# A fused attention and maxout kernel: batch 0 takes its h undivided by the sums, its weights in fp16, a recut tail of the first pass, and the next batch's h one burst later

## The chip, the cores and the metric

The kernel runs on one core of one Trainium2 chip. Time is device microseconds (us) of one execution on that core; quoted are medians with the lowest and highest of the runs. The core is TensorE (matmul), VectorE (DVE), ScalarE (ACT), GpSimd (POOL), SyncE (SP) and DMA engines.

## The reference, cut to what matters

```python
# x: [4, 12544, 128], inducing: [32, 128], w1, w2: [128, 1024], w_out: [1024, 128]
def mab(q, kv):
    s = scale * (q @ kv.transpose(0, 2, 1))        # scale = 1/sqrt(128)
    a = np.exp(s - s.max(-1, keepdims=True))
    a /= a.sum(-1, keepdims=True) + 1e-09
    return a @ kv
h = mab(I, x)                 # 32 rows per batch, from all 12544 tokens
y = mab(x, h)                 # each token attends to the 32 rows
out = np.maximum(y @ w1, y @ w2) @ w_out
```

The kernel works with max(a, b) = a + relu(b - a). So y @ w1 @ w_out becomes the attention weights times `m1 = h @ (w1 @ w_out)`, and y @ (w2 - w1) the attention weights times `hwd = h @ (w2 - w1)`. Both are small and made once a batch. In the code E is exp of the scores of the first pass, and h = (sum of E x) / (sum of E).

## The kernel before

The first batch (batch 0) is read in units of up to 16 tiles of 128 tokens: transposes, scores, exp, accumulation of E sums and of h. Then comes a long stream of bursts (hidden layer) and finals (output). The next batch's first pass runs as jobs between the bursts.

```python
    units = []
    for i, (_, n) in enumerate(p1_blocks):
        step = 8 if i == NP1 - 2 else n
        units += [(i, g, min(step, n - g)) for g in range(0, n, step)]
    units = units[:-3] + units[-1:] + units[-3:-1]
    NU = len(units)
    # ... pools, loads of x, transposes of x, u_scores (scores of a unit, exp on ScalarE) ...
        def u_accum(i):
            t, g, n = units[i]
            et = pool0.pop(("et", i))
            xn = xn_of(0, t)
            if i == 0:
                for name in ("h", "sum"):
                    pool0[name] = bank([128, 512])
                    model.bank_free[pool0[name][0]] = 1e9
            for j in range(0, n, 4):
                w = min(4, n - j) * M
                nc.tensor.matmul(
                    out=pool0["sum"][1][:, 0:w],
                    lhsT=ones16,
                    rhs=et[:, j : j + w // M, :],
                    start=(i == 0 and j == 0),
                    stop=(i == NU - 1 and j + 4 >= n),
                )
                model.pe(0.056)
            for j in range(n):
                nc.tensor.matmul(
                    out=pool0["h"][1][:, 0:M],
                    lhsT=xn[:, g + j, :],
                    rhs=et[:, j, :],
                    start=(i == 0 and j == 0),
                    stop=(i == NU - 1 and j == n - 1),
                )
                model.pe(0.025)

        def u_h():
            rec = smp.tile([C, M], F32, name="hrec_0", tag="hrec")
            nc.vector.reduce_sum(
                out=rec,
                in_=pool0["sum"][1][:, 0 : 4 * M].rearrange("p (k m) -> p m k", k=4),
                axis=mybir.AxisListType.X,
            )
            nc.vector.reciprocal(out=rec, in_=rec)
            hT4 = smp.tile([C, 4, M], F16, name="hT4_0", tag="hT4")
            nc.vector.tensor_mul(
                hT4,
                pool0["h"][1][:, None, 0:M].broadcast_to((C, 4, M)),
                rec[:, None, :].broadcast_to((C, 4, M)),
            )
            end = model.ev("DVE", 256 + 128, model.t["PE"], 0.2)
            for name in ("h", "sum"):
                model.bank_free[pool0[name][0]] = end
            st[0]["hT4"] = hT4.rearrange("c q m -> c (q m)")
        # ... scores and accumulation of the later batches, E summed on GpSimd ...
        def small_fold(b):
            acc = st[b]["eacc"]
            n = P1B // 2
            while n:
                nc.gpsimd.tensor_add(out=acc[:, 0:n, :], in0=acc[:, 0:n, :], in1=acc[:, n : 2 * n, :])
                n //= 2
            st[b]["esum"] = acc[:, 0, :]

        def small_h(b):
            es = st[b]["esum"]
            bi, ps = bank([128, 512])
            nc.tensor.matmul(out=ps[:, 0:M], lhsT=ones32, rhs=es, start=True, stop=True)
            end = model.pe(0.11, model.bank_free[bi])
            rec = smp.tile([C, M], F32, name=f"hrec_{b}", tag="hrec")
            nc.vector.reciprocal(out=rec, in_=ps[:, 0:M])
            hT4 = smp.tile([C, 4, M], F16, name=f"hT4_{b}", tag="hT4")
            nc.vector.tensor_mul(
                hT4,
                st[b]["hacc"][:, None, :].broadcast_to((C, 4, M)),
                rec[:, None, :].broadcast_to((C, 4, M)),
            )
            model.bank_free[bi] = model.ev("DVE", 256 + 128, end, 0.2)
            st[b]["hT4"] = hT4.rearrange("c q m -> c (q m)")

        def small_hwd(b):
            hwd = smp.tile([128, J], F16, name=f"hwd_{b}", tag="hwd")
            w = 256 if b == 0 else 512
            for i in range(J // w):
                bi, ps = bank([128, 512])
                sl = slice(w * i, w * (i + 1))
                nc.tensor.matmul(
                    out=ps[:, 0:w], lhsT=st[b]["hT4"], rhs=w21[:, sl], start=True, stop=True
                )
                end = model.pe(w / 2400 + 0.002, model.bank_free[bi])
                if i % 2 == 0:
                    nc.vector.tensor_copy(out=hwd[:, sl], in_=ps[:, 0:w])
                    model.bank_free[bi] = model.ev("DVE", w, end)
                else:
                    nc.scalar.copy(out=hwd[:, sl], in_=ps[:, 0:w])
                    model.bank_free[bi] = model.ev("ACT", w, end)
            st[b]["hwd"] = hwd
        # ... small_m1: m1 = hT4 x w1out, copied by ScalarE, m1d on GpSimd ...
        # ... Block.stage: scores against hT4, exp by ScalarE with the constant scale;
        #     burst: 16 matmuls of e2 against hwd, relu by DVE or ScalarE;
        #     final: relu against woutp (with m1d first), multiply by 1/denominator on DVE, store ...
        def prep_w1T():
            for g in range(2):
                bi, ps = bank([128, 512])
                for j in range(4):
                    jb = 4 * g + j
                    nc.tensor.transpose(
                        ps[:, 128 * j : 128 * (j + 1)],
                        w1f[:, 128 * jb : 128 * (jb + 1)],
                        identity32,
                    )
                    end = model.pe(0.12, model.bank_free[bi])
                nc.scalar.copy(out=w1T[:, 4 * g : 4 * g + 4, :], in_=ps)
                model.bank_free[bi] = model.ev("ACT", 512, end)
        # ...
        last = NU - 3
        for i in range(last - 1):
            u_transpose(i)
            if i >= 1:
                u_accum(i - 1)
            u_scores(i)
            keep_warm(1)
        u_transpose(last - 1)
        u_accum(last - 2)
        u_transpose(last)
        u_transpose(last + 1)
        u_scores(last - 1)
        u_transpose(last + 2)
        u_accum(last - 1)
        u_scores(last)
        u_scores(last + 1)
        u_scores(last + 2)
        for i in range(last, NU):
            u_accum(i)
        for i in range(NXN - NP1):
            load_x(1, i)
        u_h()
        for i in range(4):
            eng = nc.vector if i == 3 else nc.gpsimd
            sl = slice(256 * i, 256 * (i + 1))
            eng.tensor_sub(w21[:, sl], w2f[:, sl], w1f[:, sl])
        for i in range(NXN - NP1, NP1):
            load_x(1, i)
        prep_w1T()
        # ... blocks, stages ...
        stages[-1][0].stage()
        small_hwd(0)
        for blk in stages[-1][1:]:
            blk.stage()
        prep_w1out()
        # ... jobs: at(g, f) runs f behind burst g ...
            for s, f in ((40, small_fold), (42, small_h), (43, small_hwd), (44, small_m1)):
                at(g + s, f, nb)
```

## Time and profile before

| | before |
|---|---|
| time, median of 3 runs | 340.58 us (340.24 to 341.95) |
| span of the profiled execution | 338.5 us |
| TensorE busy | 97% |
| accumulation of batch 0 ends (called t0) | 23.62 |
| first burst on TensorE | 26.19 |
| first output multiply | 29.27 |
| TensorE dense from | 36.21 |

One can read this as a TensorE stream of about 300 us with a start in front of it. Whatever comes before the stream counts in full, and inside the stream only gaps of TensorE count. The lines for both are in the prediction. Two more views matter for the argument. The first is the list of what TensorE waited for, over the whole span of the kernel before, here the longest three of its six entries (engine line, what it waited for: us in total, times, longest):

```profile
PE ps L208 <- ACT xT L200: 1.3, 4, 0.4
PE ps L173 <- DVE warm L158: 1.2, 1, 1.2
PE ps L331 <- POOL eacc L324: 1.0, 1, 1.0
```

No wait for a DMA is in the whole list: the data of x was always there before TensorE came to it. The second view is a line of the timeline of GpSimd (start us, us, engine, line, operation, count, then the idle time before it and what ended that):

```profile
22.64 2.10 POOL L660 TENSOR_TENSOR w<-wf 128x256 f16<-128x256 f32 x3 [4.14 <-DMA wf<-in_moe_w_dram]
```

This is three quarters of w2 - w1; DVE forms the fourth. The work can't start before w2 has landed (22.50). GpSimd ends at 22.64 + 2.10 = 24.74, DVE at 25.03. The four multiplies that need one quarter each (L350) start on TensorE at 24.93, 25.04, 25.15 and 25.26, so the third quarter is 0.41 us early and the fourth only 0.23 us. I did not look at how tight this is when I predicted; the experiments come back to it.

### The profile page before, as it was taken

The numbers are of one execution on the slowest core, as the hardware profiler recorded it, in microseconds if no ns is written. First come the engines' busy times: TensorE is split into PE (matmuls) and PEld (weight loads), VectorE is DVE, ScalarE is ACT, GpSimd is POOL, SyncE is SP. The second block draws the span as 40 slices with busy tenths as digits, with TensorE's granted clock in tenths as the row PEclk, the third lists the DMA queues.
The fourth block names the chain that finished last, engine by engine and source line by source line (L and its number), as shares of the span: only waits on it lengthen the run. The fifth ranks groups of instructions, "written<-read, shape, count | busy, mean of one in ns | idle before, by whom it ended". The sixth has DMA issues, their size and how long they took to land.

```text
span 338.5 us, 14493 instructions
## 1 busy us (share of the span) xinstructions
PE 329.7 (97%) x6346; PEld 263.8 (78%) x6346; DVE 295.9 (87%) x620; ACT 269.7 (80%) x521; POOL 92.9 (27%) x164
## 2 busy tenths in 40 slices
PE   8899999999999999999999999999999999999996
PEld 3787688888768878888777878887777777878875
DVE  1348999999989999999998999999998998989994
ACT  1559988777888887787899777877899989888881
POOL 7243113454532224443242141423242100000000
PEclk9999999999999999999999999999999999999999
DMA  7999799499719985994229951212221221222222
GB/s 130 211 270 214 193 244 255 131 193 232 203 64 181 275 180 129 195 244 141 88 95 205 273 174 65 95 71 90 96 95 67 100 99 72 95 96 95 97 97 108
DMA packets 53423, 50.42 MB, mean 149 GB/s; under 512 B 41456, under 2 KB 42128, under 8 KB 53360
## 3 DMA queue, kind: packets, MB, share of 16 engines
q0 software_dynamic: 11408, 33.43, 37.0%
q1 hardware_dynamic: 41952, 16.08, 21.9%
q8 instruction: 49, 0.80, 1.0%
q14 instruction: 14, 0.11, 0.1%
HBM read 27.28 MB, written 25.69 MB: 157 GB/s over the span
## 4 chain that ended last, share of the span: by engine, by line
PE 93%; ACT 3%; DVE 1%; POOL 1%; issue 1%; DVEq 0%; POOLq 0%
PE ps L544 56%; PE ps L471 19%; PE ps L486 4%; PE ps L297 2%; PE ps L275 2%; PE ps L406 2%; PE ps L173 2%; PE ps L192 2%; ACT relu L508 1%; ACT xT L200 1%; PE ps L208 1%; PE ps L427 1%; PE ps L350 1%; DVE relu L504 1%; POOL eacc L324 1%
## 5 line engine op out<-in xcount | busy, mean ns | idle before, releaser
L508 ACT ACTIVATE relu<-ps 128x512 f16<-128x512 f32 x444 | 235.5, 601 | 43.0 <-PE ps L471 29.7
L504 DVE TENSOR_SCALAR relu<-ps 128x512 f16<-128x512 f32 x340 | 218.7, 679 | 5.3 <-PE ps L471 4.5
L544 PE MATMUL ps<-woutp,relu 128*128 128x128 f16 x3136 | 209.1, 220 | 0.0
L544 PEld LDWEIGHTS <-relu 128*128 128x128 f16 x3136 | 176.4, 98 | 29.8 <-issue 20.2
L560 DVE TENSOR_TENSOR o<-ps,rp 128x256 f32<-128x256 f32 x196 | 81.9, 418 | 16.0 <-PE ps L544 14.2
L570 POOL DMA_DIRECT2D out_dram<-o x75 | 41.1, 547 | 156.4 <-DVE o L560 108.1
L471 PE MATMUL ps<-e,hwd 32*128 32x256 f16 (+1 forms) x1632 | 82.8, 268 | 0.4
L471 PEld LDWEIGHTS <-hwd 32*128 32x128 f16 x1632 | 27.0, 92 | 19.0 <-issue 3.2
L486 PE MATMUL ps<-m,e 32*128 32x128 f16 x372 | 29.7, 214 | 0.7
L486 PEld LDWEIGHTS <-e 32*128 32x128 f16 x372 | 18.2, 92 | 7.0 <-issue 3.9
L317 POOL TENSOR_TENSOR eacc<-eacc,et 128x512 f32<-128x512 f32 (+1 forms) x18 | 18.5, 1028 | 0.3
L284 ACT ACTIVATE et<-ps 128x512 f16<-128x512 f32 (+1 forms) x21 | 11.4, 544 | 4.8 <-PE ps L275 4.8
L416 ACT ACTIVATE e<-ps 128x512 f16<-128x512 f32 (+2 forms) x30 | 14.9, 553 | 0.0
L114 POOL DMA_DIRECT2D xn<-in_x_dram x21 | 11.5, 550 | 4.7 <-DMA xn<-in_x_dram 4.1
L197 DVE COPY xT<-ps 128x1024 f16<-128x1024 f16 (+1 forms) x8 | 5.1, 642 | 8.4 <-PE ps L192 8.4
L200 ACT COPY xT<-ps 128x1024 f16<-128x1024 f16 x5 | 5.1, 1012 | 9.0 <-PE ps L192 9.0
L275 PE MATMUL ps<-inducingT,xT 128*128 128x32 f16 x294 | 10.6, 176 | 0.0
L297 PE MATMUL ps<-et,xn 128*128 128x32 f16 x294 | 10.6, 176 | 0.0
L275 PEld LDWEIGHTS <-xT 128*128 128x128 f16 x294 | 9.6, 96 | 0.0
L297 PEld LDWEIGHTS <-xn 128*128 128x128 f16 x294 | 9.5, 96 | 0.0
L173 PE MATMUL ps<-warm 128*128 128x512 f16 x22 | 7.7, 495 | 1.2 <-DVE warm L158 1.2
L406 PE MATMUL ps<-xT,hT 128*32 128x512 f16 (+2 forms) x120 | 8.7, 350 | 0.1
(65 smaller groups left out, 115.4 us busy)
## 6 DMA issues: line engine op xcount, KB each, us to landing
out_dram<-o POOLq DMA_DIRECT2D x72, 256.0 KB, 3.2
xn<-in_x_dram POOLq DMA_DIRECT2D x23, 512.0 KB, 8.9
out_dram<-o SPq DMA_DIRECT2D x24, 256.0 KB, 2.0
wf<-in_moe_w_dram POOLq DMA_DIRECT2D x2, 512.0 KB, 13.7
xn<-in_x_dram POOLq DMA_DIRECT2D x2, 256.0 KB, 13.5
out_dram<-o POOLq DMA_DIRECT2D x3, 128.0 KB, 4.7
xT<-xn SPq DMA_TRANSPOSE x21, 6.2
xn<-in_x_dram POOLq DMA_DIRECT2D x4, 64.0 KB, 9.3
```

The source lines that it names most:

```text
L275: nc.tensor.matmul(out=ps[:, j * M : (j + 1) * M], lhsT=xT_tiles[b % 2][:, k0 + j, :], rhs=inducingT, start=True, stop=True,)
L297: nc.tensor.matmul(out=ps[:, 0:M], lhsT=xn[:, j, :], rhs=et[:, j, :], start=(j == 0), stop=(j == n - 1),)
L317: nc.gpsimd.tensor_add(out=acc, in0=acc, in1=et[:, 0:n, :])
L406: nc.tensor.matmul(out=ps[32 * q : 32 * (q + 1), 0 : self.width], lhsT=st[self.b]["hT4"][:, 32 * q : 32 * (q + 1)], rhs=xT[:, q % self.g], ...
L416: nc.scalar.activation(out=self.e2[:, 0 : self.width], in_=ps[:, 0 : self.width], func=AF.Exp, scale=scale,)
L471: nc.tensor.matmul(out=ps[:, jj * w : (jj + 1) * w], lhsT=st[blk.b]["hwd"][r, 128 * jb : 128 * (jb + 1)], rhs=blk.e2[r, 128 * self.t0 : 12 ...
L486: nc.tensor.matmul(out=part.fin[q][1][:, 128 * s : 128 * (s + 1)], lhsT=part.blk.e2[r, 128 * tt : 128 * (tt + 1)], rhs=st[part.blk.b]["m1" ...
L504: nc.vector.tensor_scalar(out=dst, in0=src, scalar1=0.0, scalar2=None, op0=ALU.max)
L508: nc.scalar.activation(out=dst, in_=src, func=AF.Relu)
L544: nc.tensor.matmul(out=o, lhsT=self.relu[:, jb, q, tt, :], rhs=woutp[:, jb, :], start=False, stop=(s == 1 and jb == NJB - 1),)
L560: nc.vector.tensor_mul(self.osb[:, h : h + 2, :], ps[:, 0:256].rearrange("p (s c) -> p s c", s=2), rp.broadcast_to((128, 2, 128)),)
L570: eng.dma_start(out=outr[blk.b, :, k : k + nst, :], in_=self.osb[:, 0:nst, :])
```

## The change

The intent is a shorter path from the last data of x to the first burst, and no stall at batch 1's fold.

- **h undivided.** Batch 0's h is only multiplied by a constant 2**-14. The division by the E sums moves to where results leave PSUM: as a [128,1] scale of the exponentials and of the evictions of hwd and m1. E sums come as a column (weights E, moving operand one column of ones) in place of 128 columns.
- **fp16 weights.** w1 and w2 are loaded into fp16 tiles. The eight transposes of w1 are fp16, run while DVE scales and copies h, and leave by one DVE copy. w2 - w1 isn't formed: each hwd bank takes h x w2 and then -h x w1. The fp32 copies that later batches need are loaded and subtracted on GpSimd inside the stream.
- **Recut tail.** The last full block of batch 0 comes as 8, 4 and 4 tiles instead of 8 and 8, and the order on TensorE changes.
- **Fold later.** Batch 1's h, hwd and m1 come one burst later.
- In a final, the m1d matmuls come last.

The diff, cut to its core (some statements are put in words):

```diff
@@ units
-        step = 8 if i == NP1 - 2 else n
-        units += [(i, g, min(step, n - g)) for g in range(0, n, step)]
-    units = units[:-3] + units[-1:] + units[-3:-1]
+        if i == NP1 - 2:
+            units += [(i, 0, n // 2), (i, n // 2, n // 4), (i, n // 2 + n // 4, n // 4)]
+        else:
+            units.append((i, 0, n))
+    units = units[:-4] + units[-1:] + units[-4:-1]
+    last = NU - 4
@@ constants and loads
-    ones16 = consts.tile([128, 128], F16, name="ones16")
+    ones16 = consts.tile([128, 1], F16, name="ones16")
+    same_m = consts.tile([128, 4, M], F32, name="same_m")   # filled from identity32 by 4 DVE copies
+    sum_scale = consts.tile([128, 2], F32, name="sum_scale")  # HS and HS / scale, HS = 2**-14
-        nc.gpsimd.dma_start(out=w1f, in_=moe_w1)
-        nc.gpsimd.dma_start(out=w2f, in_=moe_w2)
+        nc.gpsimd.dma_start(out=w1h, in_=moe_w1)              # fp16 tiles of their own
+        nc.gpsimd.dma_start(out=w2h, in_=moe_w2)
@@ u_accum: E sums come out as a column
-                    out=pool0["sum"][1][:, 0:w],
-                    lhsT=ones16,
-                    rhs=et[:, j : j + w // M, :],
+                    out=pool0["sum"][1][0:w, 0:1],
+                    lhsT=et[:, j : j + w // M, :],
+                    rhs=ones16,
@@ u_h: h is only scaled by HS; the sums become two [128,1] scales
+            nc.vector.tensor_mul(
+                part, pool0["sum"][1][:, 0:1].broadcast_to((128, 2)), sum_scale
+            )
+            w1T_bank = w1T_transpose()            # 8 fp16 transposes into one bank
+            nc.tensor.matmul(out=ps[:, 0:2], lhsT=same_m..., rhs=part, start=True, stop=True)
+            nc.vector.tensor_scalar(out=hT4, in0=h broadcast to 4, scalar1=HS, ..., op0=ALU.mult)
+            nc.vector.reciprocal(out=rs, in_=ps[:, 0:2])
+            nc.scalar.mul(neg, hT4, -1.0)
+            w1T_evict(*w1T_bank)                  # one DVE copy
+            st[0]["rs"], st[0]["scale"] = rs[:, 0:1], rs[:, 1:2]
-            (reduce_sum, reciprocal, tensor_mul on DVE)
@@ u_hwd: two matmuls a bank in place of w21 = w2 - w1
+                for lhsT, rhs, first_mm in (
+                    (st[0]["hT4"], w2h, True),
+                    (st[0]["neg"], w1h, False),
+                ): ...
+            # evictions: hwd = ps * rs, banks 0 and 1 on ScalarE, 2 and 3 on DVE
@@ small_m1, stage
-            nc.scalar.copy(out=m1, in_=ps[:, 0:128])
+            if b == 0:
+                nc.scalar.mul(m1, ps[:, 0:128], st[0]["rs"])
-                    scale=scale,
+                    scale=st[self.b]["scale"],
@@ final: the two m1d matmuls of a group come behind its 16 relu matmuls
@@ order of the start
-        (8 fp32 transposes of w1 behind u_h, 2 ScalarE copies of them)
-        for i in range(4):
-            eng = nc.vector if i == 3 else nc.gpsimd
-            sl = slice(256 * i, 256 * (i + 1))
-            eng.tensor_sub(w21[:, sl], w2f[:, sl], w1f[:, sl])
+        for i in range(last - 2):
+            u_transpose(i); (u_accum(i - 1) if i >= 1); u_scores(i); keep_warm(1)
+        u_transpose(last - 2)
+        u_accum(last - 3)
+        u_transpose(last - 1)
+        u_scores(last - 2)
+        u_transpose(last)
+        u_transpose(last + 1)
+        u_scores(last - 1)
+        u_transpose(last + 2)
+        u_scores(last)
+        u_transpose(last + 3)
+        u_scores(last + 1)
+        u_accum(last - 2)
+        u_scores(last + 2)
+        u_scores(last + 3)
+        for i in range(last - 1, NU):
+            u_accum(i)
@@ jobs
+            d = 1 if b == 0 else 0
             for s, f in ((40, small_fold), (42, small_h), (43, small_hwd), (44, small_m1)):
-                at(g + s, f, nb)
+                at(g + s + (0 if f is small_fold else d), f, nb)
+        at(24, load_wf)            # w1, w2 once more, fp32, for w21 of the later batches
+        for i in range(4):
+            at(33 + 2 * i, sub_w, i)   # w21 quarter by quarter on GpSimd
```

> **What bounds the kernel now.** I read the page first, then the timeline of all engines from 0 to 40 us, then the waits of TensorE after 26 us, then the landing time of each early DMA, issue by issue. The page says that the whole is a TensorE stream with a start in front of it:
>
> ```profile
> PE 329.7 (97%) x6346; PEld 263.8 (78%) x6346; DVE 295.9 (87%) x620; ACT 269.7 (80%) x521; POOL 92.9 (27%) x164
> PE 93%; ACT 3%; DVE 1%; POOL 1%; issue 1%; DVEq 0%; POOLq 0%
> ```
>
> From 36 us to 90 us the table by stretches has PE busy 53.99 of 54.00 us; nothing off TensorE can shorten that, and the order of instructions shows that the change leaves the stream there as it is. So only the start (up to 36 us) and stalls of TensorE later are open. The waits of TensorE from 26 us to the end hold one entry worth anything:
>
> ```profile
> 90.67 0.54 POOL L570 DMA_DIRECT2D out_dram<-o  x1 [2.40 <-DVE hacc L310]
> 91.62 1.99 POOL L324 TENSOR_TENSOR eacc<-eacc 128x256 f32<-128x256 f32 x4
> 93.66 0.41 PE L331 MATMUL ps<-eacc,ones 128*128 128x32 f32 x2 [0.97 <-POOL eacc L324]
> ```
>
> The fold of batch 1's E sums on GpSimd ends at 93.61, and the matmul that needs it sits at the head of TensorE's queue from 92.69: 0.97 us lost, once. The later batches show no such wait.
>
> The start, on TensorE (and the ScalarE copy that paces a unit of 16 tiles):
>
> ```profile
> 16.69 1.01 ACT L200 COPY xT<-ps 128x1024 f16<-128x1024 f16 x1 [0.52 <-PE ps L192]
> 17.76 0.36 PE L208 MATMUL ps<-inducingT,xT 128*128 128x32 f16 x8 [0.29 <-ACT xT L200]
> 18.19 1.05 PE L192 MATMUL ps<-identity,xn 128*128 128x128 f16 x16
> 20.26 0.55 PE L208 MATMUL ps<-inducingT,xT 128*128 128x32 f16 x16
> 20.66 0.61 PE L192 MATMUL ps<-identity,xn 128*128 128x128 f16 x8
> 23.42 0.35 PE L242 MATMUL ps<-et,xn 128*128 128x32 f16 x8
> 23.62 1.07 PE L611 MATMUL ps<-identity,wf 128*128 128x128 f32 x8
> 26.19 0.40 PE L471 MATMUL ps<-e,hwd 32*128 32x128 f16 x16
> ```
>
> A unit recurs every 2.58 us (15.60 to 18.19), paced by transposes, then a 1.01 us copy, then scores. Accumulation ends at 23.62 (call it t0); the first burst starts at 26.19, 2.57 us later. From there to about 36 us evictions set the pace; ScalarE hardly stops:
>
> ```profile
> 27.02 1.09 ACT L508 ACTIVATE relu<-ps 128x512 f16<-128x512 f32 x2
> 27.99 0.41 ACT L416 ACTIVATE e<-ps 128x256 f16<-128x256 f32 x1
> 28.25 1.12 ACT L508 ACTIVATE relu<-ps 128x512 f16<-128x512 f32 x2
> 29.54 3.54 ACT L508 ACTIVATE relu<-ps 128x512 f16<-128x512 f32 x7 [0.16 <-PE ps L471]
> 32.94 1.11 ACT L416 ACTIVATE e<-ps 128x512 f16<-128x512 f32 x2
> 34.04 4.76 ACT L508 ACTIVATE relu<-ps 128x512 f16<-128x512 f32 x9
> ```
>
> x lands (issue time plus time to landing, each issue asked alone): fifth load 17.2, the two-tile one 17.55, the two halves of the last 18.8 and 20.1; w1 21.2, w2 22.5, w_out 23.9. A consumer starts some 0.2 us later.
>
> **What the Trainium skill says.** "TensorE: Matmul & The Clock Gate", Back-to-back issue gap: N/2.4 + 2.5 ns warm, with a floor near 25 ns for small N. The trace agrees: four sums of 128 columns take 11.32 to 11.54 (55 ns each), sixteen 32-column matmuls 11.54 to 11.95 (26 ns each). "ScalarE: Activation LUTs", What ACT_TABLE_LOAD costs: each [128,1] pointer operand adds about 93 ns to an ACTIVATE. Nothing in this trace has a scale of that kind, so it can't be checked before; it matters, since the change gives such a scale to the exponentials, the hwd evictions and m1 of batch 0. "DMA: Bandwidth & Descriptors", Where 436 GB/s comes from: a ceiling of 435 GB/s. x loads land 2.45 us apart for 1.05 MB of fp32 read, 428 GB/s, so x can't come earlier, and fp16 weights, still read as fp32, can't either: 0.52 MB in about 1.25 us both ways.
>
> **The change part by part.**
>
> Schedule of the last units. The loop now stops after three units and the last 16 tiles come as 8, 4, 4. I place its TensorE order on the trace's times with 56 ns a transpose, 25 ns a small matmul, 0.69 us a DVE copy of 8 tiles. The sum matmul falls from 55 to 25 ns (0.12 us a unit), but in the paced units that only widens the 0.29 us wait for the copy. Accumulation of unit 2 ends at 16.99, so the fifth unit's transposes wait for their data: 17.4 to 18.3, against 18.19 before. Scores of the fourth unit 18.3 to 18.7; two tiles to 18.81; eight tiles 19.0 to 19.45 (landed 18.8); scores of the fifth 19.48 to 19.88 (DVE, now copying both halves, is done at 19.42); four tiles to 20.10; two-tile scores 20.15; last four tiles 20.3 to 20.52 (landed 20.1); eight scores to 20.72; accumulation of the fourth unit (20 matmuls) to 21.22, scores to 21.42, the remaining accumulation of 34 tiles 1.08 us: t0 = 22.50. Against 23.62: **1.12 us** gained, about half from the transposes starting earlier and half from 25 cheaper sums and a gapless tail. The four new same_m copies delay the first DVE copy by an estimated 0.6 to 0.8 us (from 0.17 us of a small copy each), but its scores wait for ScalarE until 10.00 anyway, and the 0 to 0.2 us left vanish in the wait for data at 17.4.
>
> From t0 to the first burst. Removed: reduce, reciprocal, multiply on DVE (23.62 to 24.70) before anything could start; eight fp32 transposes (1.07); two ScalarE copies of w1T (1.07); the subtraction. Added on TensorE, in order: eight fp16 transposes 0.45, one fp32 matmul about 0.30 (the pair at 93.66 held TensorE 0.34), scores 0.18, eight hwd matmuls of 256 columns 0.86 (four before), second scores 0.18, eight w1out 0.45. Sum 2.42 against 2.57. The chain beside it: part 0.17, matmul result at t0+0.85, reciprocal to t0+1.05, exp to 1.5, two ScalarE hwd evictions to 2.3, DVE w1T copy 0.69 and two hwd evictions to 2.54; the third pass of the burst needs that at 2.6. So TensorE work replaces the wait: **0.15 us**, first DVE relu at t0+2.85 against t0+3.02. On ScalarE hwd, the second exp, w1out and m1, each with a pointer, put the first relu at t0+3.56 against t0+3.40. In all, 0.
>
> Start of the stream. Four scaled activations (m1, three exps before 34 us) at 0.09 us add up to 0.36 us to a ScalarE that doesn't stop; DVE is near as full. I count 0.15 us lost. m1d matmuls last in a final: its group waits for relu anyway (28.06 after 27.99), so 0.
>
> Fold one burst later. A burst and its final take 1.3 to 1.5 us; 92.69 + 1.4 = 94.1, after the fold's 93.61. The four 0.72 us subtractions move to GpSimd between bursts 33 and 39, where it idles 1.0 to 2.4 us at a time, so the fold isn't late: **0.97 us** gained whole.
>
> Sum: 1.12 + 0 - 0.15 + 0.97 = 1.95 us, so 340.58 - 1.95 = 338.6 us.
>
> **The rivals.** First, x's arrival takes the place of TensorE's order: the last four tiles land at 20.1, and if quarter loads land later by 0.5 us, t0 moves to 23.0 and the time to 339.1. Against it: they are read at the same rate. Second, ScalarE becomes the bound from t0 to 36 us, because every pointer costs its full 0.09 us and m1 comes later: 0.5 us more, 339.1. For it: the lines from 27.02 on. Third, the gain on the path is larger, with DVE setting the first evictions (0.17 us) and the pointers hidden behind overlap of back-to-back activations: 338.2. Fourth, the fold stall comes back at the new place because the subtractions or the second weight load hold GpSimd up: 339.5. The idle times before 90.67 speak against it. Fifth, the transposes of batch 1 by DMA: they wait for x that lands at 39.1 while the step now comes at 39.0, scores at 45.6 need a transpose that takes 4.6 us from 39.5: about 1.4 us of slack, no cost.
>
> **Range and chances.** Rivals one, two and four in part together leave a gain of about 0.9; the good ends together give 2.9. I take 337.7 to 339.7. Two per cent is 6.8 us, beyond anything in the start, so faster by that 0.01, within 0.985, slower 0.005.
>
> **What would show it.** Fifth unit's transposes near 17.4; first w1T transpose near 22.5; first burst at 24.9, TensorE without a gap before it; ScalarE's first relu near 26.0; no TensorE wait for the fold. A t0 above 23, a new DMA wait before the last transposes, or scaled exps holding banks so that the stream gets dense later than 35.3 would make it wrong.

## The result, and the profile after

| | before | after |
|---|---|---|
| time, median of 6 runs each of the same rounds | 340.92 us (340.24 to 341.95) | 339.04 us (338.44 to 339.95) |
| ratio | | 0.9945 (95% interval 0.9923 to 0.9966) |
| span of the profiled execution | 338.5 us | 336.9 us |
| t0 | 23.62 | 22.69 |
| first burst | 26.19 | 25.38 |
| first output multiply | 29.27 | 28.54 |
| TensorE dense from | 36.21 | 35.49 |

A ratio is the mean time of one kernel's fast runs over that of the other's fast runs of the same rounds, so not quite the ratio of the medians that I quote. All runs were in the fast state. The verdict is "same" at 2%. The medians lie 1.88 us apart, the predicted difference was 1.95 us, and 339.04 lies in the predicted range.

The chain of work that ended last, from the changed kernel's page:

```profile
PE 90%; DMA 4%; POOL 1%; ACT 1%; DVE 1%; issue 1%; POOLq 0%
```

DMA is new in that chain with 4% of 336.9 us, about 13 us: the start is now followed back to the loads of x and not to ScalarE, which had 3% before. The list of TensorE's waits in the changed kernel says the same (its entries for `warm` and `mask`, which the kernel before has too, are left out):

```profile
PE ps L218 <- DVE xT L207: 1.1, 1, 1.1
PE ps L218 <- ACT xT L210: 0.8, 2, 0.4
PE ps L202 <- DMA xn<-in_x_dram: 0.6, 1, 0.6
PE ps L555 <- ACT relu L592: 0.4, 2, 0.2
```

The wait for the fold is gone from it, a wait for x has come. The 1.1 us for a DVE copy is in the first unit and lies in front of that wait for x, so it costs nothing. It comes from the four new same_m copies, which took 0.91 us at 7.70 in front of that copy (0.6 to 0.8 were predicted).

The start of the changed kernel, from the timeline of TensorE:

```profile
17.38 1.07 PE L202 MATMUL ps<-identity,xn 128*128 128x128 f16 x16 [0.65 <-DMA xn<-in_x_dram]
...
22.69 0.61 PE L264 MATMUL ps<-identity,w1h 128*128 128x128 f16 x8
23.14 0.34 PE L283 MATMUL ps<-sum_part,same_m 128*128 128x2 f32 x2
23.51 0.24 PE L490 MATMUL ps<-xT,hT 128*32 128x128 f16 x4
23.68 0.28 PE L399 MATMUL ps<-w2h,hT 128*128 128x256 f16 x1
...
24.83 0.62 PE L699 MATMUL ps<-woutp,w1T 128*128 128x128 f16 x8
25.38 0.40 PE L555 MATMUL ps<-e,hwd 32*128 32x128 f16 x16
```

The fifth unit's transposes come as its data does, at 17.38 (17.4 was predicted). t0 is the first transpose of w1, at 22.69. From there to the first burst TensorE is hardly idle, and still takes 25.38 - 22.69 = 2.69 us, more than the 2.57 us before. In those 2.69 us the eight transposes run to 23.14, the fp32 matmul of the sums and an idle moment behind it (see e8_tuned) last to 23.51, the eight hwd matmuls run to 24.66 (0.98 us), the second scores to 24.83, w1out to 25.38 (0.55 us).

The fold of batch 1 in the changed kernel, on GpSimd and TensorE, and below it the burst that followed the fold's matmul in the kernel before:

```profile
90.97 1.99 POOL L364 TENSOR_TENSOR eacc<-eacc 128x256 f32<-128x256 f32 x4
92.38 1.07 PE L619 MATMUL ps<-woutp,relu 128*128 128x128 f16 x16
93.29 0.36 PE L371 MATMUL ps<-eacc,ones 128*128 128x32 f32 x2
93.58 0.40 PE L555 MATMUL ps<-e,hwd 32*128 32x256 f16 x8
```

```profile
94.00 0.40 PE L471 MATMUL ps<-e,hwd 32*128 32x256 f16 x8
```

The fold ends at 90.97 + 1.99 = 92.96. The matmul that needs it now stands behind one more burst and final and starts at 93.29, with no idle time before it. From the start of the final ahead of the fold's matmul to the burst behind it, the changed kernel takes 93.58 - 92.38 = 1.20 us; the kernel before took 94.00 - 91.63 = 2.37 us for the same work. That is 1.17 us, more than the 0.97 us that the profile calls idle, because an idle time is counted from a modelled end of the matmuls.

To see where the time went I compare the start of every output multiply on DVE, of which each kernel has 196, one against the other (after less before):

| output multiply (numbered from 0) | time before | difference |
|---|---|---|
| 0 | 29.27 | -0.73 |
| 34 | 87.01 | -0.72 |
| 38 | 92.96 | -0.68 |
| 44 | 104.30 | -1.86 |
| 101 | 193.99 | -1.81 |
| 195 (last) | 335.35 | -1.95 |

There are two steps and no more. 0.72 us come from the start, and 1.86 - 0.68 = 1.18 us from the place of the fold. The last -0.14 is not the change's: the profile of the kernel before hesitates once at about 196 us (multiply 102), and the traces of e1_fold to e4_schedfold below hold the same -0.15 or so against it there, whatever they change. The span shrinks by 1.6 us only, since the last store ended 3.5 us behind the last multiply after and 3.1 us before.

### The profile page after: what moved, and what is told of

Same layout as the page of the kernel before. It is cut to its first block, busy times and chain, and to the rows that moved or that the text cites. A ratio compares the mean times of both kernels' runs of the same rounds, so it can differ in the third digit from the quotient of the medians.

```text
span 336.9 us, 14513 instructions
## 1 busy us (share of the span) xinstructions
PE 327.8 (97%) x6351; PEld 262.9 (78%) x6351; DVE 296.7 (88%) x627; ACT 269.6 (80%) x521; POOL 94.4 (28%) x166
## 3 DMA queue, kind: packets, MB, share of 16 engines
q1 hardware_dynamic: 42240, 17.13, 25.7%
## 4 chain that ended last, share of the span: by engine, by line
PE 90%; DMA 4%; POOL 1%; ACT 1%; DVE 1%; issue 1%; POOLq 0%
PE ps L619 57%; PE ps L555 19%; PE ps L570 4%; DMA xn<-in_x_dram 4%; PE ps L337 2%; PE ps L315 2%; PE ps L490 2%; ACT relu L592 1%; POOL xn L123 1%; DVE o L645 1%; PE ps L511 1%; DVE relu L588 1%; PE ps L252 0%; PE ps L431 0%; PE ps L628 0%
## 5 line engine op out<-in xcount | busy, mean ns | idle before, releaser
L207 DVE COPY xT<-ps 128x1024 f16<-128x1024 f16 (+2 forms) x10 | 5.7, 596 | 6.8 <-PE ps L202 6.6
L500 ACT ACTIVATE e<-ps 128x512 f16<-128x512 f32 (+1 forms) x21 | 10.9, 581 | 0.0
L210 ACT COPY xT<-ps 128x1024 f16<-128x1024 f16 x4 | 4.0, 1012 | 7.8 <-PE ps L202 7.8
L490 PE MATMUL ps<-xT,hT 128*32 128x512 f16 (+2 forms) x120 | 8.7, 350 | 0.0
L202 PE MATMUL ps<-identity,xn 128*128 128x128 f16 x98 | 6.9, 219 | 1.0 <-DMA xn<-in_x_dram 0.6
```

Source lines behind the costliest of these rows:

```text
L490: nc.tensor.matmul(out=ps[32 * q : 32 * (q + 1), 0 : self.width], lhsT=st[self.b]["hT4"][:, 32 * q : 32 * (q + 1)], rhs=xT[:, q % self.g], ...
```

## The experiments

The theory was: (1) the fold's place alone gives about 1 us or a little more; (2) the start gives some 0.7 us, and what sets it is the arrival of x, the order on TensorE behind it, and then TensorE's own work up to the first burst. Rivals: the gain comes from the rewritten arithmetic alone or the new cut alone; the [128,1] scales cost their full length; the order in the final matters. Differences in us below are (1 - ratio) times the median of the kernel before of the same call. In the first call that median was 340.35 us (340.10 to 340.82, 11 runs), in the second 340.74 (340.22 to 342.26, 11 runs), in the fourth, on a noisier chip, 341.48 (340.30 to 343.04, 11 runs). Some runs have a mean granted clock of 0.995 or less and are 0.5 to 4 us longer than their like: two of the 11 of the kernel before in the second call (342.21 and 342.26) and in the fourth (342.72 and 343.04), two of e11_split's six, and one each of e8_tuned's and e12_tunedsplit's. They count as fast, and are in the ratios. In the second call they raise the mean of the kernel before, and with it every difference, by 0.27 us.

This table gathers what the traces show of each kernel's start. "Multiply 0" and "195" are the times of the first and last output multiply against the same trace of the kernel before.

| kernel | first transposes | t0 | first burst | t0 to burst | multiply 0 | 195 |
|---|---|---|---|---|---|---|
| before | 7.84 | 23.62 | 26.19 | 2.57 | 0 | 0 |
| after | 7.19 | 22.69 | 25.38 | 2.69 | -0.73 | -1.95 |
| e1_fold | 8.09 | 23.88 | 26.45 | 2.57 | +0.26 | -1.07 |
| e2_nofold | 7.05 | 22.70 | 25.46 | 2.76 | -0.64 | -0.76 |
| e3_sched | 8.65 | 23.09 | 25.93 | 2.84 | -0.27 | -0.39 |
| e4_schedfold | 8.27 | 22.72 | 26.00 | 3.28 | -0.20 | -1.53 |
| e5_rewrite | 7.08 | 22.80 | 25.59 | 2.79 | -0.51 | -1.80 |
| e6_nosub | 8.24 | 22.68 | 25.35 | 2.67 | -0.84 | -1.54 |
| e7_imm | 8.37 | 22.83 | 25.80 | 2.97 | -0.40 | -1.68 |
| e8_tuned | 6.70 | 22.44 | 25.39 | 2.95 | -0.72 | -1.95 |
| e9_after | 7.90 | 22.71 | 25.97 | 3.26 | -0.14 | -1.37 |
| e10_m1dfirst | 8.30 | 22.80 | 25.75 | 2.95 | -0.35 | -0.36 |
| e11_split | 8.49 | 23.76 | 27.81 | 4.05 | +1.70 | +1.27 |
| e12_tunedsplit | 6.89 | 23.19 | 25.77 | 2.58 | -0.34 | -1.57 |

The second column must be read first. The warming matmuls at the head of the kernel run at a lower rate until the clock opens, 376 to 634 ns for one and the same 512-column matmul in one trace, and when it opens differs from run to run. The traces' granted clock becomes 1.00 at 4.24 us in after, 5.55 in before and 7.19 in e3_sched, and over the 12 traces with 18 warming matmuls the first transposes follow in the same order, between 7.05 and 8.65 (7.19 and 7.90 in two traces of the same changed kernel). The 6.70 and 6.89 of e8_tuned and e12_tunedsplit have 14 warming matmuls. In the kernel before TensorE paces all that follows: t0 comes 15.78 us behind the first transposes in before (23.62 - 7.84) and 15.79 in e1_fold (23.88 - 8.09). In the changed kernel t0 stays at 22.69 to 22.83 over five traces (after, e2, e7, e9, e10) with first transposes from 7.05 to 8.37: its early units have idle time that takes up a late start, and its fifth unit waits for x when the start was early (0.65 us in the first trace, 0.27 in e9's, none in e7's and e10's). So the pair before and after is not a fair one: the clock opened 1.31 us sooner in after. The fair pair is before and e9_after, whose clock opened at 5.66.

### e1_fold: the fold's place alone

The kernel before with only this:

```diff
+            d = 1 if b == 0 else 0
             for s, f in ((40, small_fold), (42, small_h), (43, small_hwd), (44, small_m1)):
-                at(g + s, f, nb)
+                at(g + s + (0 if f is small_fold else d), f, nb)
```

> Kernel before with nothing changed but batch 1's sums used one burst later. Theory (the removed wait of 0.97 us and a second one right behind it are worth 1.1 us of the 1.9): 1.1 us faster than before, TensorE waits nowhere for the fold, the start is as before. Rival (the gain is all in the start; the wait is made up later, since TensorE runs in a regime where evictions had got ahead): 0.0 to 0.3 us faster.

Measured: 338.94 us (338.80 to 339.26, 5 runs), ratio 0.9960 (0.9948 to 0.9971), 1.36 us faster. In its trace the wait for the fold is gone: the fold ends at 91.87 + 1.99 = 93.86 and the matmul starts at 94.21. The multiplies go from +0.25 ahead of the fold to -0.94 behind it, a step of 1.19 us, the same as the changed kernel's. So the fold's step is shown to stand by itself.

### e2_nofold: the change without the fold's new place

```diff
-            d = 1 if b == 0 else 0
+            d = 0
```

> Changed kernel with the sums of batch 1 used at the old burst again. Theory: 1.0 to 1.2 us slower than the changed kernel, so 0.7 to 0.9 us faster than before; a wait of about 1 us at the fold's matmul comes back. Rival (start is everything): within 0.3 us of the changed kernel, 1.6 to 1.9 us faster than before.

Measured: 340.08 us (339.41 to 340.70, 6 runs), ratio 0.9991 (0.9978 to 1.0004), 0.3 us faster, which can't be told apart from no change and is less than both texts expected. The list of TensorE's waits has the old one back:

```profile
PE ps L371 <- POOL eacc L364: 1.0, 1, 1.0
```

In its trace the start gains 0.64 us, in the mean of its runs 0.3. The trace had its first transposes at 7.05, and a kernel before that starts as early should gain with it (no run shows one); a single pair of traces therefore says too much or too little about the start, and the mean over runs is the better judge.

### e3_sched: the new cut and order alone

The kernel before with the hunks of the units and of the order of the start, and nothing else:

```diff
-    units = units[:-3] + units[-1:] + units[-3:-1]
+    units = units[:-4] + units[-1:] + units[-4:-1]      # last block as 8, 4, 4
+    (order of transposes, scores and accumulation as in the change)
```

> Kernel before with the new cut (8, 4, 4) and order of the last units alone; h divided as before, sums of 128 columns. Theory (the start's gain of 0.7 us is the schedule): fifth unit's transposes near 17.4 us, accumulation ends near 23.0 to 23.1, first burst near 25.6 to 25.7, 0.5 to 0.6 us faster than before. Rival (the start's gain is the undivided h with its cheap sums): under 0.2 us faster.

Measured: 340.25 us (339.82 to 340.50, 5 runs), ratio 0.9994 (0.9982 to 1.0006): no gain told. But t0 came 14.44 us behind the first transposes (23.09 - 8.65), 1.34 us sooner than the 15.78 before. This was the gain that I expected of the recut tail, and more, and the first burst did not take it over: it came 2.84 us after t0, at 25.93 where 25.6 to 25.7 was expected.

### e4_schedfold: cut, order and the fold

e3_sched with the edit of e1_fold.

> Kernel before with schedule and later fold, without the undivided h, fp16 weights and w1T on DVE. Theory: 1.6 to 1.7 us faster than before, 0.2 to 0.3 us slower than the changed kernel, as the undivided h shortens nothing after the accumulation. Rival (undivided h is what shortens the start): 1.1 us faster than before or less, 0.8 us slower than the changed kernel.

Measured: 338.78 us (338.59 to 338.87, 5 runs), ratio 0.9952 (0.9940 to 0.9965), 1.6 us faster: e1's 1.36 and e3's 0.2 added. Its trace shows who keeps the burst. From its timeline, GpSimd and TensorE:

```profile
22.63 2.28 POOL L666 TENSOR_TENSOR w<-wf 128x256 f16<-128x256 f32 x3 [3.17 <-DMA wf<-in_moe_w_dram]
24.97 0.38 PE L353 MATMUL ps<-w,hT 128*128 128x256 f16 x2 [0.46 <-POOL w L666]
26.00 0.40 PE L474 MATMUL ps<-e,hwd 32*128 32x128 f16 x16
```

t0 is 22.72, 0.90 us before the kernel before's, but w2 - w1 still starts when w2 has landed and ends at 24.91. The multiply waits 0.46 us for it, and the first burst comes at 26.00. A recut tail can't pay while this subtraction stands on the path.

### e5_rewrite: the change with the old cut and order

```diff
-            units += [(i, 0, n // 2), (i, n // 2, n // 4), (i, n // 2 + n // 4, n // 4)]
+        step = 8 if i == NP1 - 2 else n
+        units += [(i, g, min(step, n - g)) for g in range(0, n, step)]
     (and the old order of the start)
```

> Changed kernel with the old cut (8, 8) and order of the last units; undivided h, fp16 weights and later fold kept. Theory (schedule and rewrite pay only together): burst starts about 2.7 us after the accumulation ends, accumulation ends 15.5 to 15.8 us after the first transpose; 0.1 to 0.3 us faster than the kernel before with the later fold alone (so 1.4 to 1.6 us faster than before), 0.2 to 0.5 us slower than the changed kernel. Rival (the rewrite carries the start's gain alone): as fast as the changed kernel.

Measured: 339.75 us (338.66 to 340.68, 6 runs), ratio 0.9961 (0.9935 to 0.9986), 1.3 us faster. The runs fall into two groups, three at 338.7 to 339.2 and three at 340.3 to 340.7. t0 came 15.72 us behind the first transposes (22.80 - 7.08), as in the kernel before (15.78): the rewritten arithmetic alone doesn't shorten the part up to t0. The early t0 of this trace is its early clock. In the mean its gain is that of the fold (1.36) and nothing more, with the wide interval that the two groups give.

### e6_nosub: e4_schedfold without the subtraction, wrong on purpose

```diff
-        nc.gpsimd.dma_start(out=w2f, in_=moe_w2)
+        nc.gpsimd.dma_start(out=w21, in_=moe_w2)        # w2 straight in the place of w2 - w1
-        for i in range(4):
-            ... tensor_sub(w21[:, sl], w2f[:, sl], w1f[:, sl])
```

The result is wrong on purpose (relative error 0.71); every other instruction stays.

> Schedule and later fold on the kernel before, with w2 loaded in fp16 where w2 - w1 was computed (a wrong result on purpose): the subtraction on GpSimd and its wait are gone, all else stands. Theory (what held the first burst in the run with schedule and fold was the subtraction, 0.5 us of wait at the hwd matmuls): first burst 2.6 us after the accumulation ends instead of 3.28, 0.4 to 0.7 us faster than that run by the trace, about as fast as the changed kernel. Rival (chain through reduce, reciprocal and multiply sets it): 0.0 to 0.2 us.

Measured: 338.60 us (338.13 to 339.08, 6 runs), ratio 0.9928 (0.9906 to 0.9949), 2.5 us faster than before, the fastest of all. t0 is 22.68 (22.72 in e4), and the first burst is 0.65 us sooner:

```profile
25.35 0.40 PE L474 MATMUL ps<-e,hwd 32*128 32x128 f16 x16
```

So the subtraction alone held e4's burst. And here is what the undivided h is worth: the old chain (reduce, reciprocal and multiply on DVE, fp32 transposes) without the subtraction needs 2.67 us from t0 to the burst, the new chain at its best trace 2.69. The new arithmetic doesn't shorten that stretch by much (2.58 in e12_tunedsplit is its best); it removes a subtraction that would have become the bound. This trace hesitates by 0.5 us in all between 78 and 92 us; what is seen of it is said under e11_split.

### e9_after: the changed kernel once more

> The changed kernel once more, on the chip of these runs, as their measure. 1.6 to 1.9 us faster than before. First transposes anywhere from 7.0 to 8.7 us; if at 8.0 or earlier, the fifth unit's still start at 17.4 (data), else 9.4 us after the first.

Measured: 338.73 us (338.51 to 339.81, 6 runs), ratio 0.9939 (0.9918 to 0.9959), 2.1 us faster, as in the first measurement (0.9945). But its trace gains only 0.14 us at the start. Its fifth unit starts at 17.72 and not at the expected 17.4, since that load of x landed at 17.67 (17.33 in the first trace). t0 is hardly touched by it (22.71), but there is a wait that the first trace had not:

```profile
24.09 0.24 PE L490 MATMUL ps<-xT,hT 128*32 128x128 f16 x4 [0.60 <-DVE rs L301]
```

DVE's rs (the reciprocal) is named as releaser, but the scores of this line use x and the undivided h, not rs. Something else held TensorE for 0.60 us at this point. I looked for it in e8_tuned, e7_imm and e10_m1dfirst and then tested it with e11_split.

### e7_imm: constants in place of the [128,1] scales, wrong on purpose

```diff
-                    nc.scalar.mul(hwd[:, sl], ps[:, 0:w], st[0]["rs"])
+                    nc.scalar.mul(hwd[:, sl], ps[:, 0:w], 1.25)
-                nc.scalar.mul(m1, ps[:, 0:128], st[0]["rs"])
+                nc.scalar.mul(m1, ps[:, 0:128], 1.25)
-                    scale=st[self.b]["scale"],
+                    scale=scale,
```

The result is wrong on purpose (relative error 0.022).

> Changed kernel with constants in place of every [128,1] scale on ScalarE in batch 0: exponentials, two hwd evictions, m1 (a wrong result on purpose). Prediction's term (four scaled activations cost the start of the stream 0.15 us, up to 0.36): from first burst to the first dense final (the first 16 final matmuls after which TensorE no longer waits) 9.75 to 9.95 us against 10.11, the activations each 0.05 to 0.1 us shorter. Rival (the pointer's cost is hidden by the overlap of activations in a row): their records shorter, the stretch 10.05 to 10.15.

Measured in one run, state unknown: 338.94 us, beside 340.45 us of the kernel before. Two groups of the changed kernel, by form (count, busy us, mean ns of one), first with the scale from memory and then with a constant:

```profile
L500 ACT ACTIVATE e<-ps,rs 128x128 f16<-128x128 f32 x3 | 1.1, 371 | 0.3 <-PE ps L490 0.3
L500 ACT ACTIVATE e<-ps 128x128 f16<-128x128 f32 x3 | 0.9, 298 | 0.0
```

and the hwd evictions of the changed kernel:

```profile
L421 ACT ACTIVATE hwd<-ps,rs 128x256 f16<-128x256 f32 x2 | 0.8, 469 | 0.0
```

and of e7_imm:

```profile
L421 ACT ACTIVATE hwd<-ps 128x256 f16<-128x256 f32 x2 | 0.7, 380 | 0.0
```

One scale from memory costs 73 ns in the first pair and 89 ns in the second. On the path they come to far less: from the first burst to the dense stream e7_imm takes 35.82 - 25.80 = 10.02 us, the changed kernel 35.49 - 25.38 = 10.11. All of them together cost 0.09 us. This lies between what the theory and the rival expected. e7_imm is one trace, but the stretch hardly scatters: it takes 10.11 us in each of the eight traces with these scales and 10.02 in each of the six without (before, e1, e3, e4, e6, e7), of which only e7 differs from the changed kernel in nothing else.

### e10_m1dfirst: the m1d matmuls first in a final, as before

```diff
+                    if start:
+                        nc.tensor.matmul(out=o, lhsT=blk.e2[...], rhs=st[blk.b]["m1d"][:, q, :], start=(s == 0), ...)
                     for jb in range(NJB):
                         ...
-                if start:
-                    (the m1d matmuls behind the relu matmuls)
```

> Changed kernel with the m1d matmuls first in a final again. Prediction: first relu group, not m1d, is what the first final waits for, so first burst to first output multiply stays at 3.16 us, within 0.06. Rival: m1d holds the first final up, 0.2 us or more later.

Measured in one run, state unknown: 340.27 us. From the first burst to the first multiply it takes 28.92 - 25.75 = 3.17 us, the changed kernel 3.16; from the burst to the dense stream 10.11 both. The order in the final is worth nothing. The time is no better than before's because this execution lost 1.3 us in one stretch from 82 to 94 us, which the two traces of the changed kernel don't show (see e11_split for a part of it); so its time decides nothing and its start does.

### e8_tuned: an attempt at a better start

The changed kernel with fewer warming matmuls (14, not 18), the same_m copies behind the first unit, and the accumulation of the fourth unit drawn ahead into TensorE's idle time:

```diff
-        keep_warm(18)
+        keep_warm(14)
-        (same_m copies ahead of the first unit)
+        (behind its transposes)
         u_scores(last)
+        u_accum(last - 2)
         u_transpose(last + 3)
         u_scores(last + 1)
-        u_accum(last - 2)
         u_scores(last + 2)
+        u_accum(last - 1)
```

> Changed kernel with 14 warming matmuls for 18, same_m built after the first unit's transposes, and accumulation of the fourth unit ahead of the last four tiles' transposes. Theory (the start swings with the time at which the clock opens during warming, and TensorE is left idle 0.2 us before the last tiles): first transposes at 6.9 to 7.3 us, accumulation ends near 22.4 instead of 22.7; 0.2 to 0.4 us faster than the changed kernel, smaller spread. Rival (the clock opens later with less warming and the start gets slower): 0.3 us or more slower.

Measured: 338.92 us (338.67 to 339.89, 6 runs), ratio 0.9943 (0.9922 to 0.9963): not faster than the changed kernel. t0 did come 0.25 us sooner (22.44), but the first burst came at 25.39 as in the changed kernel:

```profile
23.69 0.28 PE L399 MATMUL ps<-w2h,hT 128*128 128x256 f16 x1 [0.30 <-DMA w2h<-in_moe_w_dram]
```

The trace puts the 0.30 us down to the load of w2, which landed at 23.47. There was a second candidate, the same as for e9_after's 0.60 us. The kernel's instructions are themselves fetched by DMA, in a queue of their own: 49 packets of 16 KB, together 0.80 MB, beside TensorE's 12,702 matmuls and weight loads (some 63 bytes of that queue's traffic for each, so about 256 to a packet by this estimate). At the start one packet comes every 6 us or so.

Number TensorE's matmuls and weight loads from 0 in the order in which they start. In each trace of the changed kernel and its kin, number 702 starts 2.3 to 2.4 us behind the start of a packet, whether TensorE is idle there or not: 2.32 (after), 2.41 (e2), 2.35 (e5), 2.30 (e7), 2.29 (e8), 2.41 (e9), 2.29 (e10). In the changed kernel number 702 belongs to the first of the scores at L490, which is where e9_after was idle for 0.60, e7_imm for 0.32 and e10_m1dfirst for 0.30 us. e8_tuned has eight instructions fewer ahead of these scores, and there number 702 belongs to the first hwd matmul, which is where it waited. (The expectation of e11_split says 699; counted in the packed traces it is 702.)

### e11_split: each 512-column warming matmul as four of 128 columns

If TensorE waits for its instructions at a fixed number, more instructions ahead of it move the wait to another place in the program.

```diff
-                nc.tensor.matmul(out=ps, lhsT=warm[:, 0:128], rhs=warm, start=True, stop=True)
+                for c in range(0, 512, 128):
+                    nc.tensor.matmul(out=ps[:, c : c + 128], lhsT=warm[:, 0:128], rhs=warm[:, c : c + 128], start=True, stop=True)
```

This puts 126 more instructions ahead of the scores, for the same columns.

> Changed kernel with each warming matmul of 512 columns as four of 128: 126 TensorE instructions more ahead of the first scores, the same array time. Theory (TensorE's instructions come in 16 KB packets, 256 instructions each; one such border lies at the first scores of batch 0, number 699 of TensorE's list, and they start 2.3 to 2.6 us after that packet in all runs, 0.0 to 0.6 us late): the border moves to earlier work, no idle time before the first scores whatever the start, which follow the same_m matmul by 0.30 us; first burst 2.6 to 2.7 us after the accumulation ends in this trace, median up to 0.3 us faster than the changed kernel's 338.73 (against before: 2.0 to 2.3 us). Rival (the wait there is something else, such as a result's semaphore): 0.3 to 0.6 us of idle time stays there when the first transposes start at 7.9 us or later.

Measured: 339.53 us (338.94 to 342.24, 6 runs), ratio 0.9953 (0.9914 to 0.9993). The idle time in front of the first scores is gone (L290 at 24.52, its scores at 24.98, at a lower clock), and a new one stands in the middle of an accumulation, where no semaphore is waited for:

```profile
22.23 0.21 PE L259 MATMUL ps<-et,xn 128*128 128x32 f16 x2 [0.64 <-issue]
```

Fourteen of sixteen matmuls of the fourth unit ran, then 0.64 us of nothing, then the last two. Counted in the same way, the wait again stands in front of instruction 702, 2.19 us behind the start of the packet (20.04). So the wait follows the instruction count and not the data. As an improvement it failed: the stall moved and stayed. In this trace TensorE then ran at a lower clock up to about 27.3 us (hwd matmuls 0.21 us apart in place of 0.11; the granted clock is 0.50 from 23.85 to 27.27), which puts its first burst at 27.81, and not 2.6 to 2.7 us behind t0 as expected. That is one trace; what lowered the clock is open.

Going on from 702 in steps of 256, and taking one packet for each step, there are 674 such places in the 14 traces. None starts less than 2.19 us behind its packet, and most are far behind theirs and show no idle time. Part of the later hesitations stands at such places too: e10_m1dfirst was idle for 0.19 us just ahead of number 3006 (82.67, 2.43 us behind the packet) and e11_split for 0.36 us ahead of number 1982 (57.98, 2.59 us). In e6_nosub three of them between 76 and 90 us come 2.27 to 2.49 us behind their packets, with 0.28 us idle near the third. The rest of what these traces lost there stays unexplained.

### e12_tunedsplit: e8_tuned with the same split

> The tuned kernel (14 warmings, same_m later, accumulation of the fourth unit earlier) with the split warmings. Theory: the 0.30 us before the hwd matmuls, put down to w2, was the same border, shifted by the eight instructions removed; it is gone, first burst near 25.05 us, 2.2 to 2.5 us faster than before. Rival (w2's landing at 23.5 is real): hwd still starts at 23.6 to 23.7, burst at 25.4.

Measured: 339.50 us (338.45 to 342.96, 6 runs), ratio 0.9956 (0.9915 to 0.9998): not faster. The idle time again stands inside an accumulation, now of the fifth unit, and again in front of instruction 702:

```profile
22.05 0.41 PE L259 MATMUL ps<-et,xn 128*128 128x32 f16 x10 [0.31 <-issue]
```

The hwd matmuls run at 24.07 right behind the scores, without e8's wait. But they run 0.38 us later than in e8, and w2 landed at 22.93 here, so this doesn't separate the two candidates for e8's 0.30 us. Neither expectation came: the first burst was at 25.77. Without the stall ahead of it, the stretch from t0 to the burst takes 25.77 - 23.19 = 2.58 us, the shortest of the rewritten kernels.

No version beat the changed kernel by more than the spread of the runs. e6_nosub is wrong.

## Why the prediction was right, and where it was not

**The total** was right: 1.88 us measured (1.95 predicted), 339.04 in a range from 337.7 to 339.7. e9_after repeated it with 2.1 (1.8 without the two runs of the kernel before at a lower clock). The terms of the sum are off by more than the sum is: in the profile pair the start gave 0.25 us less than predicted and the fold 0.21 us more. That they cancelled to 0.07 us is luck.

| term | predicted | profile pair | what the runs add |
|---|---|---|---|
| accumulation ends earlier (t0) | 1.12 | 0.93 | 0.79 to 0.93 over five traces, against before's one |
| from t0 to the first burst | 0 | -0.12 | -0.12 to -0.69 |
| start of the stream (scales) | -0.15 | -0.09 | all scales together 0.09 |
| fold one burst later | 0.97 | 1.18 | 1.19 in e1's trace, 1.36 in its time |

The first three give 0.93 - 0.12 - 0.09 = 0.72, which is the step of the multiplies at the start. By the prediction's own sign this part was wrong: a stream that gets dense later than 35.3 was to show that, and it got dense at 35.49. The first burst was forecast at 24.9 and came at 25.38.

The start's size is also less sure than the pair makes it look. In the fair pair (before and e9_after) t0 comes 0.91 us sooner and the first multiply only 0.14. In the times, the changed kernel's 1.9 less e1_fold's 1.36 leaves about 0.5 us, and the intervals of the two ratios overlap (0.9923 to 0.9966 and 0.9948 to 0.9971). So the fold's gain is shown, and the start's gain points one way but is not clear of the noise.

**t0.** That x's arrival would take over as the gate, at 17.4, was right to 0.02 us (17.38). The rest of the tail took 22.69 - 17.38 = 5.31 us, where I had placed 5.1; small items were left out, such as the sum of a two-tile unit, which holds TensorE for 0.13 us (22.00 to 22.13) in place of 0.025. I gave about half of the 1.12 to earlier transposes; by my own times they were 0.79 of it (18.19 to 17.4), and 0.81 were measured. The ceiling of 435 GB/s that the prediction sets beside x's 428 is, on the page cited there, one of the ports of the on-chip memory, while 428 counts fp32 bytes read and the page of the kernel before shows about half as many moved. So the closeness of the two numbers proves nothing; that x came no sooner is shown by its fifth load, which landed at 17.16 before, 17.33 after and 17.67 in e9_after. What I had not seen is that before's t0 isn't a constant: it hangs on when the clock opens. Against a kernel before that starts early, less is won.

**From t0 to the first burst** is the step that failed. I wrote "TensorE work replaces the wait: 0.15 us", and the stretch grew in place of shrinking. My 2.42 us were made of durations that were too short: hwd 0.98 for 0.86, w1out 0.55 for 0.45, and 0.37 from the fp32 matmul to the scores for 0.30. These three add up to 0.29, against 0.27 by which the stretch was longer. The first two could be read in the trace of the kernel before: w1out took 0.55 there (25.64 to 26.19), and four hwd matmuls 0.53. The third is not the fp32 matmul's: where instruction 702 lies elsewhere the step takes 0.27 (22.88 to 23.15 in e8, 23.63 to 23.90 in e12), so 0.10 of it goes to the fetch of instructions. On top comes, in four of the six other traces of rewritten kernels that keep the warming matmuls whole, a larger loss (e9: 0.57 more than in the first trace), of which the idle time at instruction 702 is the part seen (0.30 to 0.60). I never thought of the fetch of instructions.

**What the start's gain consists of** was told wrongly. I split it into earlier transposes and cheaper sums. e3 and e4 show that the recut tail moves t0 by itself, to 22.72, without any of the new arithmetic, and e5 that the new arithmetic alone doesn't move it. e6 against e4 shows that the arithmetic's worth is w2 - w1, which leaves the path of the first burst: 0.65 us at the burst. Neither half alone shows a gain in the times (e3 0.2 us; e5 no more than the fold's). Both together show 0.3 in e2 and about 0.5 as the changed kernel's 1.9 less e1's 1.36, neither clear of the noise. I had listed the subtraction under "removed" and given it no time.

**The scales** cost what was expected for each record (73 to 89 ns) and less on the path. The rival of a ScalarE bound (0.5 us more) did not come about: taking all scales out gave 0.09 us (e7, and the other traces without them). **m1d last** was rightly put at 0 (e10). **same_m** took 0.91 us, and disappeared in the wait for x as predicted.

**The fold** went as told, with the subtractions in GpSimd's gaps and no new wait; it was undersized by 0.2 us. The wait was put at the 0.97 us that the profile calls idle; from the final ahead of it to the burst behind it TensorE took 2.37 us, and 1.20 once the wait was gone. That is 1.17 of the 1.18.

**Left open:** most of what single traces lose later (0.5 us in e6 and 1.3 in e10 between 78 and 94 us, 0.8 in e11 between 50 and 60); why the clock opens late in some runs; whether e8's 0.30 us was w2 (23.69 is 0.22 us behind its landing) or the instructions (2.29 us behind their packet); and why the packets of instructions came late enough to stall in some traces and not in others.

## What to carry to other kernels

Before shortening a path, list everything that arrives at its end and by how little each is hidden: here a recut that won 0.9 us at t0 was worth nothing alone, because a subtraction off the critical path ended only 0.2 to 0.4 us ahead of its use. Where one program's start moves by a microsecond from run to run, judge a part by the mean of its runs and by the time behind a fixed event, not by one pair of traces. And a matmul delayed by a slower engine needs no faster engine if one independent burst can be put in front of it: that one line was most of the gain.

## What the Trainium skill lacked or had wrong

- "Runtime: NRT & Kernel Launch", Instruction fetch mechanics, says that instructions come in 16 KiB blocks of 256 and that crossing a block's border is mostly hidden. The traces agree on the blocks (49 packets, 0.80 MB). They show that it isn't hidden in a dense stretch of small matmuls: TensorE stood idle at the border at its instruction 702 for 0.30 to 0.64 us in six of the traces (e7, e8, e9, e10, e11, e12, of which e8's has a second candidate), with the packet 2.2 to 2.4 us ahead. The page gives no time for a crossing.
- "ScalarE: Activation LUTs", What ACT_TABLE_LOAD costs, gives about 93 ns for a [128,1] pointer operand. Measured were 73 ns on 128 columns and 89 ns on 256, and all of them together cost only 0.09 us of the path. The page says that activations in a row overlap by about 93 ns; how much of a scale's cost is left among other work it doesn't say.
- "TensorE: Matmul & The Clock Gate", Weight-path perf modes, ties fast weight loads to 128 weights. For fewer the page has only its rule for a weight load (columns / 1.2 ns, so an estimated 53 ns for 64). A one-column matmul with 64 columns of weights held TensorE for 0.13 us (22.00 to 22.13 in the changed kernel, 23.07 to 23.20 in e11_split), where those with 128 columns came 0.025 us apart.
- "TensorE: Matmul & The Clock Gate", What's actually happening, says that the opening of the clock varies from run to run, and puts the loss at under 1% of a typical span. It lacks what this does to a comparison: over the 12 traces with 18 warming matmuls the first transposes came between 7.05 and 8.65 us, 1.6 us apart, where the whole change is worth 1.9 us (0.55%).
